# An output product as seven half-size float32 products in place of eight, in a fused mLSTM and SwiGLU kernel

## The chip, the cores and the metric

The kernel runs on one core of a Trainium2 chip. The metric is the device time of one execution in microseconds (us), the median over several runs; lower is better. All arithmetic of the block that is changed is float32.

## The reference

The first half is an mLSTM cell with 4 batches, 8 heads, 768 steps and head size 40; its result is laid out as 3072 tokens of 320 features. The second half, which the change touches, is a SwiGLU block over these tokens:

```python
# x: (3072, 320)   w_gate, w_val: (320, 1536)   w_out: (1536, 320)
g = x @ w_gate
silu = g * (1.0 / (1.0 + np.exp(-g)))
val = x @ w_val
return (silu * val @ w_out).astype(np.float32)
```

## The kernel before

The 768 steps are cut into six groups of 128 steps (`g` = 0 to 5). A group holds 128 steps of each of the 4 batches, so 512 tokens. For every group the kernel does three things on TensorE, in an order that is written out by hand (no scheduler moves instructions):

- **Hidden layer**, `hidden(g, m)` for m = 0 to 11: 128 of the 1536 inner features for all 512 tokens, gate and value side by side in two PSUM banks (line 651). ScalarE takes the silu into a tile `sg` (line 656, two buffers), VectorE multiplies by the value and writes `h_sb` (line 657). `h_sb` holds 13 blocks of 128 features by 512 tokens, and `hid` walks round these 13, so that a group writes other blocks than the last one.
- **mLSTM work of the next group** (`n` = g + 1), put between the hidden blocks by the table `slots`: scores, state, output of the cell, and, in slots 8 and 10, `send_squares`: 32 small DMAs that move the cell's result to `x_sq`, from where VectorE turns it into the next group's `xT` (`turn_inputs`, line 426, four instructions).
- **Output product**, `project(g, u)` for the four batches u: twelve float32 multiplications in a chain over the twelve feature blocks, each with 128 tokens as the stationary operand and 320 outputs as the moving one (line 667). ScalarE copies the bank out (line 661), SyncE sends it (line 662).

A float32 multiplication is executed as two TensorE passes, so the profile counts 2 MATMUL and 2 LDWEIGHTS records for each. Group 0's output product (`project_all`, line 674) is arranged differently and the change leaves it alone; with "the five later groups" g = 1 to 5 is meant.

Between the four `project` calls stands other work that runs on other engines. For f = g + 2 below 6 (g = 1 to 3) the decay weights `w_sb` are made ready: they are loaded by SyncE (line 447, slot 9), VectorE subtracts (`weights_sub`, line 451, two instructions), GpSimd masks (line 456, four), ScalarE takes exponents (line 460), GpSimd weighs the values (line 341). The four `turn_inputs` stand there too, for g = 1 to 4:

```python
        for u in range(B):
            if f < NG and u < 2:
                weights_sub(f, u)
                weights_mask(u)
...
            if n < NG and u >= 2:
                turn_inputs(n, 2 * u - 4)
                turn_inputs(n, 2 * u - 3)
            project(g, u)
```

Every engine works through its own instructions in the order in which the program issues them, and SyncE's DMA queue does so too. PSUM has four banks for the hidden layer and the output product (tag `gen`) and four for the cell.

Of the kernel before, what the change touches and what calls it, by code (L numbers as in the profile page):

```python
# [9 lines left out]
F32 = mybir.dt.float32  # L10
# [4 lines left out]
ALU = mybir.AluOpType  # L15
# [3 lines left out]
L = 128  # L19
# [5 lines left out]
def kernel(  # L25
# [18 lines left out]
    nc = tc.nc  # L44
    B, H, S, D = q.shape
    BH = B * H
    NG = S // L
# [5 lines left out]
    DM, DF = moe_w_gate.shape  # L53
    NFC = DF // 128
    TW = B * L
# [4 lines left out]
    NH = NFC + 1  # L60
# [6 lines left out]
    work = ctx.enter_context(tc.tile_pool(name="work", bufs=2))  # L67
# [8 lines left out]
    def bank(name, tag="cell"):  # L76
        return psum.tile([128, 512], F32, name=name, tag=tag)

    def half(i):
        return slice(i * SUB, (i + 1) * SUB)  # L80
# [5 lines left out]
    def heads(P):  # L86
        return slice(P * UH, (P + 1) * UH)
# [13 lines left out]
    wo_sb = const.tile([128, NFC, DM], F32)  # L101
    h_sb = const.tile([128, NH, TW], F32)
# [237 lines left out]
    def weigh_values(eng, P):  # L340
        eng.tensor_tensor(vw_sb[:, heads(P)], v_sb[:, heads(P)], w_sb[:, heads(P), last].to_broadcast([128, UH, D1]),  # L341
                          op=ALU.mult)
# [82 lines left out]
    def turn_inputs(n, u):  # L425
        nc.vector.transpose(out=xT(n)[:, :, ts(u, L)], in_=x_sq[:, u * NKC:(u + 1) * NKC].rearrange("p w t d -> p w (t d)"))  # L426

    def xT(n):
        return xTs[max(n - 1, 0) % 2]
# [19 lines left out]
    def weights_sub(n, P):  # L449
        gb = g_T[:, n, heads(P)].unsqueeze(2).to_broadcast([128, UH, SUB])  # L450
        nc.vector.tensor_tensor(w_sb[:, heads(P)], gb, w_sb[:, heads(P)], op=ALU.subtract)  # L451

    def weights_mask(P):
        for i in range(2):
            w = w_sb[half(i), heads(P)]
            nc.gpsimd.affine_select(w, w, compare_op=ALU.is_ge, fill=NEG, base=0, pattern=[[0, UH], [1, SUB]],  # L456
                                    channel_multiplier=-1)

    def weights_exp(P):
        nc.scalar.activation(w_sb[:, heads(P)], w_sb[:, heads(P)], AF.Exp)  # L460

    def sig(P):
        nc.scalar.activation(o_sb[:, heads(P)], o_sb[:, heads(P)], AF.Sigmoid)
# [10 lines left out]
    A, V, G = nc.scalar, nc.vector, nc.gpsimd  # L474
# [166 lines left out]


    def hid(g, m):
        return h_sb[:, (g * NFC + m) % NH, :]

    def hidden(g, m, first=()):
        ps = [bank("gv_ps", "gen") for _ in range(2)]
        x = xT(g)
        for kc in range(NKC):
            for i in range(2):  # L650
                nc.tensor.matmul(ps[i], lhsT=wgv_sb[half(i), m, PAIRS[kc][i] if g < 2 else kc, :], rhs=x[half(i), kc, :],  # L651
                                 start=(kc == 0), stop=(kc == NKC - 1))
        for f in first:
            f()
        sg = work.tile([128, TW], F32, name="sg")
        nc.scalar.activation(sg, ps[0], AF.Silu)  # L656
        nc.vector.tensor_tensor(hid(g, m), sg, ps[1], op=ALU.mult)  # L657

    def result(g, u, p):
        z = work.tile([128, DM], F32, name="z_sb")  # L660
        nc.scalar.copy(z, p)  # L661
        nc.sync.dma_start(out=out[ds(u * S + g * L, L), :], in_=z)

    def project(g, u):
        p = bank("o_ps", "gen")[:, 0:DM]
        for m in range(NFC):
            nc.tensor.matmul(p, lhsT=hid(g, m)[:, ts(u, L)], rhs=wo_sb[:, m, :], start=(m == 0), stop=(m == NFC - 1))  # L667
        result(g, u, p)

    def project_all(g, after):  # L670
        ps = [bank("o_ps", "gen")[:, 0:DM] for _ in range(B)]
        for m in range(NFC):
            for u in range(B):
                nc.tensor.matmul(ps[u], lhsT=hid(g, m)[:, ts(u, L)], rhs=wo_sb[:, m, :], start=(m == 0),  # L674
                                 stop=(m == NFC - 1))
            for f in after.get(m, ()):
                f()
        for u in range(B):
            result(g, u, ps[u])

    live = {}

# [41 lines left out]
    run = lambda f, *a, **b: (lambda: f(*a, **b))  # L724
# [29 lines left out]
    def early_squares(part):  # L754
# [17 lines left out]
        11: [run(early_squares, 1)],  # L772
    }
    project_all(0, after)
    early_scope.close()
    late = ctx.enter_context(tc.tile_pool(name="late", bufs=1))
# [2 lines left out]
    k_sq = late.tile([128, PP, L // SQ, SQ], F32, name="k_sq")  # L779
    nc.gpsimd.memset(k_sq, 0.0)  # L780
    x_sq = late.tile([128, B * NKC, L // SQ, SQ], F32, name="x_sq")


    for g in range(1, NG):
        n, f = g + 1, g + 2
        slots = {m: [] for m in range(NFC)}
        if n < NG:
            if n > 2:
                slots[0] = [run(turn_squares, q_sq, qT)]
                slots[1] = [run(turn_squares, k_sq, kT)]  # L790
            slots[3] = [run(do_scores), run(do_weigh, 0)]
            slots[4] = [run(do_weigh, 1)]
            slots[4].append(run(do_decayed, 2 * n))
            slots[5] = [run(do_add, n), run(do_state, 2 * n)]
            slots[7] = [run(do_attend, n, 0), run(do_gather, n, 0)]
            slots[8] = [run(do_divide, n, 0), run(send_squares, 0)]
            slots[9] = [run(do_attend, n, 1), run(do_gather, n, 1)]
            slots[10] = [run(do_divide, n, 1), run(send_squares, 1)]
        if f < NG:
            slots[2] += [run(load_squares, q_sq, q, f), run(load_squares, k_sq, k, f)]  # L800
            slots[5].append(run(load_all, k_sb, k, f))
            slots[9] += [run(load_all, v_sb, v, f), run(weights_load, f)]
            slots[10].append(run(load_all, o_sb, o_gate, f))
        for m in range(NFC):
            hidden(g, m)
            for s in slots[m]:
                s()
        for u in range(B):
            if f < NG and u < 2:
                weights_sub(f, u)  # L810
                weights_mask(u)
            if f < NG and u == 2:
                weights_exp(0)
                weights_exp(1)
                sig(0)
                sig(1)
                weigh_values(nc.gpsimd, 0)
                weigh_values(nc.gpsimd, 1)
            if n < NG and u >= 2:
                turn_inputs(n, 2 * u - 4)  # L820
                turn_inputs(n, 2 * u - 3)
            project(g, u)


# [28 lines left out]
```

## Time and profile before

| | |
|---|---|
| median of 3 runs | 551.57 us (551.15 to 551.81) |
| span of the profiled execution | 550.0 us |
| TensorE matmul busy | 544.9 us, 99% of the span |
| VectorE, ScalarE, GpSimd busy | 236.1, 136.1 and 103.0 us |
| hidden layer, line 651 | 316.6 us busy, 1440 matmul records |
| output product of groups 1 to 5, line 667 | 130.5 us busy, 480 matmul records |
| output product of group 0, line 674 | 26.9 us busy, 96 matmul records |
| DMA | 45.69 MB, 83 GB/s mean |

No total time is recorded for the profiled execution itself; its span is 1.6 us (0.3%) under the median of the timed runs, which also hold what lies around the span.

A row of the costliest groups reads: line, engine, operation, written tile, read tiles, shapes (for TensorE rows of the array times columns of the array, then the moving operand), the number of records, then busy time and the mean duration of one record in ns, then the idle time ahead of them. PEld is TensorE's loading of the stationary operand. Records of neighbouring matmuls overlap, since the profile's duration of one covers its way through the array; so the pace is read from the distance between starts. A line of the timeline gives start and length in us of a run of like instructions, how many there are, and in brackets how long the engine sat idle before and for whom.

### The profile page before, as it was taken

How to read it: one execution, taken by the hardware profiler on the slowest of the kernel's cores; microseconds unless marked ns; L12 is line 12 of the kernel's file. 1: busy time of each engine (PE TensorE's matmuls, PEld its weight loads, DVE VectorE, ACT ScalarE, POOL GpSimd, SP SyncE). 2: the span in 40 equal slices, each digit the busy share in tenths (PEclk: the TensorE clock that was granted, in tenths of full speed). 3: DMA queues.
4: the chain of work that ended last, by engine and by line, in shares of the span. 5: the costliest groups of instructions: out<-in, count | busy, mean ns of one | idle time of the engine just before them, and what ended most of it. 6: DMA issues, size and time to landing. Idle time of an engine off the chain costs nothing.

```text
span 550.0 us, 11592 instructions
## 1 busy us (share of the span) xinstructions
PE 544.9 (99%) x4989; PEld 311.4 (57%) x4989; DVE 236.1 (43%) x397; ACT 136.1 (25%) x203; POOL 103.0 (19%) x95
## 2 busy tenths in 40 slices
PE   8999999999999999999999999999999999999997
PEld 4964556774555575545575545576455567444475
DVE  5778668961346232455421545531436621111100
ACT  4376755352110133011024101115110100111100
POOL 2304265673011060011133011124001100000000
PEclk9999999999999999999999999999999999999999
DMA  9999997878431762660564551395000131000000
GB/s 123 177 294 184 188 277 154 146 104 118 53 49 23 120 112 64 74 74 11 87 117 104 63 72 14 59 146 113 1 1 2 32 63 40 12 1 0 2 24 24
DMA packets 223994, 45.69 MB, mean 83 GB/s; under 512 B 214504, under 2 KB 219112, under 8 KB 223944
## 3 DMA queue, kind: packets, MB, share of 16 engines
q1 hardware_dynamic: 222036, 42.11, 46.7%
q10 hardware_dynamic: 1908, 2.85, 1.9%
q8 instruction: 39, 0.64, 0.5%
q14 instruction: 11, 0.09, 0.1%
HBM read 35.68 MB, written 4.01 MB: 72 GB/s over the span
## 4 chain that ended last, share of the span: by engine, by line
PE 98%; DVE 1%; ACT 0%; issue 0%; ACTq 0%; DVEq 0%
PE gv_ps L651 57%; PE o_ps L667 24%; PE o_ps L674 5%; PE inter L377 2%; PE sp L331 2%; PE intra L382 2%; PE add L353 1%; PE first_y L530 1%; PE burn L469 1%; PE tp_kq L509 1%; PE sp L519 1%; PE wps L480 0%; PE tp_kq L296 0%; PE wps L484 0%; PE wps L489 0%; PE tp_x L439 0%
## 5 line engine op out<-in xcount | busy, mean ns | idle before, releaser
L651 PE MATMUL gv_ps<-xT,wgv_sb 64*128 64x512 f32 x1440 | 316.6, 593 | 0.3 <-DVE wgv_sb L207 0.3
L651 PEld LDWEIGHTS gv_ps<-xT,wgv_sb 64*128 64x128 f32 x1440 | 138.1, 187 | 159.1 <-issue 156.4
L657 DVE TENSOR_TENSOR h_sb<-sg,gv_ps 128x512 f32<-128x512 f32 x72 | 49.5, 688 | 212.3 <-ACT sg L656 212.3
L667 PE MATMUL o_ps<-wo_sb,h_sb 128*128 128x320 f32 x480 | 130.5, 433 | 0.0
L667 PEld LDWEIGHTS o_ps<-wo_sb,h_sb 128*128 128x128 f32 x480 | 90.8, 190 | 41.0 <-issue 3.8
L656 ACT ACTIVATE sg<-gv_ps 128x512 f32<-128x512 f32 x72 | 43.0, 597 | 263.7 <-PE gv_ps L651 263.7
L456 POOL TENSOR_SCALAR_AFFINE_SELECT w_sb<-w_sb 64x1024 f32<-64x1024 f32 x20 | 28.5, 1423 | 63.9 <-DVE w_sb L451 62.9
L362 POOL TENSOR_TENSOR C<-C,dec 128x328 f32<-128x328 f32 x20 | 14.5, 738 | 134.8 <-DVE C L369 134.8
L661 ACT COPY z_sb<-o_ps 128x320 f32<-128x320 f32 x24 | 10.0, 423 | 93.2 <-PE o_ps L667 89.4
L403 POOL TENSOR_TENSOR o_sb<-o_sb,y_sb 128x640 f32<-128x640 f32 x10 | 14.2, 1431 | 78.9 <-DVE y_sb L394 78.9
L674 PE MATMUL o_ps<-wo_sb,h_sb 128*128 128x320 f32 x96 | 26.9, 437 | 0.0
L451 DVE TENSOR_TENSOR w_sb<-g_T,w_sb 128x1024 f32<-128x1024 f32 x10 | 13.1, 1354 | 28.6 <-DMA w_sb<-M_dram 28.6
L426 DVE STREAM_TRANSPOSE xT<-x_sq 128x640 f32<-128x640 f32 x16 | 12.5, 822 | 22.9 <-DMA x_sq<-x_sb 22.9
L674 PEld LDWEIGHTS o_ps<-wo_sb,h_sb 128*128 128x128 f32 x96 | 17.9, 190 | 7.2
L394 DVE TENSOR_TENSOR y_sb<-y_sb,intra 64x328 f32<-64x328 f32 x40 | 19.7, 492 | 0.7
L369 DVE TENSOR_TENSOR C<-C,add 40x328 f32<-40x328 f32 (+1 forms) x36 | 17.7, 493 | 1.2 <-POOL C L362 0.6
L377 PEld LDWEIGHTS inter<-C,qT 64*64 64x64 f32 x640 | 10.2, 134 | 7.3 <-issue 6.1
L460 ACT ACTIVATE w_sb<-w_sb 128x1024 f32<-128x1024 f32 x10 | 10.6, 1058 | 12.7 <-POOL w_sb L456 12.7
L207 POOL TENSOR_TENSOR wgv_sb<-wgv_sb,low 128x640 int32<-128x640 int32 x6 | 9.3, 1546 | 23.5 <-DVE wgv_sb L200 23.5
L341 POOL TENSOR_TENSOR vw_sb<-v_sb,w_sb 128x656 f32<-128x656 f32 x10 | 12.8, 1306 | 0.4
L338 DVE TENSOR_TENSOR w_sb<-sp,w_sb 128x512 f32<-128x512 f32 x20 | 12.7, 682 | 0.0
L397 DVE TENSOR_SCALAR den<-den 128x16 f32<-128x16 f32 x10 | 12.2, 1215 | 0.3
(132 smaller groups left out, 344.5 us busy)
## 6 DMA issues: line engine op xcount, KB each, us to landing
w_sb<-M_dram SPq DMA_DIRECT2D x10, 512.0 KB, 7.3
x_sq<-x_sb SPq DMA_DIRECT2D x128, 40.0 KB, 2.0
k_sb<-in_k_dram SPq DMA_DIRECT2D x12, 320.0 KB, 6.0
v_sb<-in_v_dram SPq DMA_DIRECT2D x12, 320.0 KB, 5.6
o_sb<-in_o_gate_dram SPq DMA_DIRECT2D x12, 320.0 KB, 5.5
raw<-in_moe_w_out_dram SPq DMA_DIRECT2D x3, 1280.0 KB, 7.5
out_dram<-z_sb SPq DMA_DIRECT2D x24, 160.0 KB, 1.8
q_sb<-in_q_dram SPq DMA_DIRECT2D x32, 64.0 KB, 2.3
```

What stands on the lines that cost most here:

```text
L362: nc.gpsimd.tensor_tensor(state(s + 1)[:, a], state(s)[:, a], dec[:, s - 2, a].unsqueeze(2).to_broadcast([128, UA, D1]), op=ALU.mult)
L369: nc.vector.tensor_tensor(c, c, ps[r], op=ALU.add)
L377: nc.tensor.matmul(inter[two][half(i), a, :], lhsT=qT[half(two), P * UA + a, half(i)], rhs=state(2 * n + i)[half(two), P * UA + a, :], sta ...
L394: nc.vector.tensor_tensor(t, t, intra[i][half(c)], op=ALU.add)
L403: eng.tensor_tensor(o, o, y[:, :, 0:D], op=ALU.mult)
L451: nc.vector.tensor_tensor(w_sb[:, heads(P)], gb, w_sb[:, heads(P)], op=ALU.subtract)
L456: nc.gpsimd.affine_select(w, w, compare_op=ALU.is_ge, fill=NEG, base=0, pattern=[[0, UH], [1, SUB]], channel_multiplier=-1)
L651: nc.tensor.matmul(ps[i], lhsT=wgv_sb[half(i), m, PAIRS[kc][i] if g < 2 else kc, :], rhs=x[half(i), kc, :], start=(kc == 0), stop=(kc == N ...
L656: nc.scalar.activation(sg, ps[0], AF.Silu)
L657: nc.vector.tensor_tensor(hid(g, m), sg, ps[1], op=ALU.mult)
L667: nc.tensor.matmul(p, lhsT=hid(g, m)[:, ts(u, L)], rhs=wo_sb[:, m, :], start=(m == 0), stop=(m == NFC - 1))
L674: nc.tensor.matmul(ps[u], lhsT=hid(g, m)[:, ts(u, L)], rhs=wo_sb[:, m, :], start=(m == 0), stop=(m == NFC - 1))
```

## The change

In groups 1 to 5 the output product is no longer four chains of twelve multiplications with 320 output columns. Tokens (batches 0 and 1 against 2 and 3), inner features (blocks 0 to 5 against 6 to 11) and outputs (columns 0 to 159 against 160 to 319) are each halved. The plain way then has eight half-size products; the new function `project_seven` computes seven products of sums of halves and adds the results up (a form of Strassen's and Winograd's scheme). Each product is 6 feature blocks times 2 batches, so 12 multiplications with a 128 by 128 stationary operand and 160 moving columns.

What is added for it:

- `out_weights`, once on GpSimd after group 0: three tiles of weight sums `wT`, and a difference in place in `wo_sb`.
- `out_sums(k)`, six times in each group on GpSimd, after hidden blocks 6 to 11: a sum into `S_lo` (or the thirteenth block of `h_sb`) and a difference in place of the second token half of block k.
- `out_second` and `out_fourth`, in each group three VectorE instructions each, which change the sums in place between the products that use them. The fifth product in the order of issue (`"b"`) reads what `out_second` writes, the seventh (`"d"`, second time) what `out_fourth` writes.
- Four VectorE additions, one on GpSimd and three ScalarE copies that put the results together, in place of four ScalarE copies; eight half-size output DMAs in place of four. Two `sg` buffers hold the partial results `u2` and `v`.

`hid` now gives block m in every group. The weights' and inputs' preparation is put between the seven products by `before`.

```diff
     def hid(g, m):
-        return h_sb[:, (g * NFC + m) % NH, :]
+        return h_sb[:, m, :]
-    def project(g, u):
-        p = bank("o_ps", "gen")[:, 0:DM]
-        for m in range(NFC):
-            nc.tensor.matmul(p, lhsT=hid(g, m)[:, ts(u, L)], rhs=wo_sb[:, m, :], start=(m == 0), stop=(m == NFC - 1))
-        result(g, u, p)
+    def out_weights(eng):
+        lo, hi = wo_sb[:, 0:KH], wo_sb[:, KH:]
+        n1, n2 = slice(0, NW), slice(NW, DM)
+        eng.tensor_tensor(wT[:, 0], lo[:, :, n2], lo[:, :, n1], op=ALU.subtract)
+        eng.tensor_tensor(wT[:, 1], hi[:, :, n2], wT[:, 0], op=ALU.subtract)
+        eng.tensor_tensor(wT[:, 2], hi[:, :, n1], wT[:, 1], op=ALU.subtract)
+        eng.tensor_tensor(lo[:, :, n2], hi[:, :, n2], lo[:, :, n2], op=ALU.subtract)
+    def out_sums(k, eng):
+        eng.tensor_tensor(s_sum(k), h_sb[:, k, second_half], h_sb[:, KH + k, second_half], op=ALU.add)
+        eng.tensor_tensor(h_sb[:, k, second_half], h_sb[:, k, first_half], h_sb[:, k, second_half], op=ALU.subtract)
+    def out_second(eng):
+        for j in range(KH // 2):
+            eng.tensor_tensor(s_pair(j), s_pair(j), h_sb[:, 2 * j:2 * j + 2, first_half], op=ALU.subtract)
+    def out_fourth(eng):
+        for j in range(KH // 2):
+            eng.tensor_tensor(s_pair(j), h_sb[:, KH + 2 * j:KH + 2 * j + 2, first_half], s_pair(j), op=ALU.subtract)
+    def project_seven(g, before):
...
+        def product(x, lhs, rhs, start, stop):
+            for k in range(KH):
+                for i in range(2):
+                    nc.tensor.matmul(node[x][:, i], lhsT=lhs(k)[:, ts(i, L)], rhs=rhs(k), start=start and k == 0 and i == 0,
+                                     stop=stop and k == KH - 1, skip_group_check=True)
...
+        step(0)
+        product("a", a11, lambda k: wo_sb[:, k, n1], True, False)
+        nc.scalar.copy(u2, node["a"])
+        step(1)
+        product("c", a21, lambda k: wo_sb[:, k, n2], True, False)
+        nc.scalar.copy(v, node["c"])
+        step(2)
+        product("d", s_sum, lambda k: wT[:, 0, k], True, False)
+        nc.vector.tensor_tensor(v, v, node["d"], op=ALU.add)
+        out_second(nc.vector)
+        step(3)
+        product("a", a12, lambda k: wo_sb[:, KH + k, n1], False, True)
+        z = fresh()
+        nc.scalar.copy(z, node["a"])
+        send(z, 0, n1)
+        step(4)
+        product("b", s_sum, lambda k: wT[:, 1, k], True, True)
+        nc.vector.tensor_tensor(u2, u2, node["b"], op=ALU.add)
+        out_fourth(nc.vector)
+        nc.gpsimd.tensor_tensor(v, v, u2, op=ALU.add)
+        send(v, 2, n2)
+        step(5)
+        product("c", a22, lambda k: wT[:, 2, k], False, True)
+        z = fresh()
+        nc.vector.tensor_tensor(z, u2, node["c"], op=ALU.add)
+        send(z, 2, n1)
+        step(6)
+        product("d", s_sum, lambda k: wo_sb[:, KH + k, n2], False, True)
+        nc.vector.tensor_tensor(u2, u2, node["d"], op=ALU.add)
+        send(u2, 0, n2)
...
+    out_weights(nc.gpsimd)
...
         for m in range(NFC):
             hidden(g, m)
+            if m >= KH:
+                out_sums(m - KH, nc.gpsimd)
...
+        before = {i: [] for i in range(7)}
+        if f < NG:
+            before[0] += [run(weights_sub, f, 0), run(weights_mask, 0)]
+            before[2] += [run(weights_sub, f, 1), run(weights_mask, 1)]
+            before[4] += [run(weights_exp, 0), run(weights_exp, 1), run(sig, 0), run(sig, 1),
+                          run(weigh_values, G, 0), run(weigh_values, G, 1)]
+        if n < NG:
+            before[4] += [run(turn_inputs, n, 0), run(turn_inputs, n, 1)]
+            before[6] += [run(turn_inputs, n, 2), run(turn_inputs, n, 3)]
+        project_seven(g, before)
```

More of the change, by code (lines that the diff above doesn't have):

```diff
@@ L679, in project_all, with s_sum, s_pair @@
             result(g, u, ps[u])
+    KH = NFC // 2
+    NW = DM // 2
+    TH = TW // 2
+    first_half, second_half = slice(0, TH), slice(TH, TW)
+    def s_sum(k):
+        return S_lo[:, k] if k < 4 else h_sb[:, NFC].rearrange("p (k t) -> p k t", t=TH)[:, k - 4]
+    def s_pair(j):
+        return S_lo[:, 2 * j:2 * j + 2] if j < 2 else h_sb[:, NFC].rearrange("p (k t) -> p k t", t=TH)
+    def out_weights(eng):
[5 more added lines that the diff above has]
+        eng.tensor_tensor(lo[:, :, n2], hi[:, :, n2], lo[:, :, n2], op=ALU.subtract)
@@ new lines, in project_seven, with send, fresh, step @@
+    def project_seven(g, before):
+        n1, n2 = slice(0, NW), slice(NW, DM)
+        a11 = lambda k: h_sb[:, k, first_half]
+        a12 = lambda k: h_sb[:, KH + k, first_half]
+        a21 = lambda k: h_sb[:, k, second_half]
+        a22 = lambda k: h_sb[:, KH + k, second_half]
+        node = {x: bank("o_ps", "gen")[:, 0:DM].rearrange("p (u d) -> p u d", d=NW) for x in "acdb"}
+        kept = {x: work.tile([128, TW], F32, name="sg")[:, 0:DM].rearrange("p (u d) -> p u d", d=NW) for x in "uv"}
+        def send(z, u, n):
+            for i in range(2):
+                nc.sync.dma_start(out=out[ds((u + i) * S + g * L, L), n], in_=z[:, i])
+        def fresh():
+            return work.tile([128, DM], F32, name="z_sb").rearrange("p (u d) -> p u d", d=NW)
+        def product(x, lhs, rhs, start, stop):
+            for k in range(KH):
+                for i in range(2):
+                    nc.tensor.matmul(node[x][:, i], lhsT=lhs(k)[:, ts(i, L)], rhs=rhs(k), start=start and k == 0 and i == 0,
+                                     stop=stop and k == KH - 1, skip_group_check=True)
+        def step(n):
+            for f in before.get(n, ()):
+                f()
+        u2, v = kept["u"], kept["v"]
+        step(0)
[28 more added lines that the diff above has]
+        send(u2, 0, n2)
@@ L781 @@
     x_sq = late.tile([128, B * NKC, L // SQ, SQ], F32, name="x_sq")
+    wT = late.tile([128, 3, KH, NW], F32, name="wT")
+    S_lo = late.tile([128, 4, TH], F32, name="S_lo")
+    out_weights(nc.gpsimd)
     for g in range(1, NG):
@@ L805 @@
             hidden(g, m)
+            if m >= KH:
+                out_sums(m - KH, nc.gpsimd)
             for s in slots[m]:
                 s()
[L808 to L822, printed above, removed]
+        before = {i: [] for i in range(7)}
[8 more added lines that the diff above has]
+        project_seven(g, before)
 _INS = ['q', 'k', 'v', 'i_gate', 'f_gate', 'o_gate', 'moe_w_gate', 'moe_w_val', 'moe_w_out']
```

## The prediction

> **What bounds the kernel now.** I read the page first: busy shares, the clock by slices, and the chain of work that ended last.
>
> ```profile
> PE 544.9 (99%) x4989; PEld 311.4 (57%) x4989; DVE 236.1 (43%) x397; ACT 136.1 (25%) x203; POOL 103.0 (19%) x95
> PEclk9999999999999999999999999999999999999999
> PE 98%; DVE 1%; ACT 0%; issue 0%; ACTq 0%; DVEq 0%
> ```
>
> TensorE is the bound, without gaps and at full clock, so TensorE time taken away counts in full unless TensorE then has to wait. The groups by cost give the row that changes and its weight loads:
>
> ```profile
> L667 PE MATMUL o_ps<-wo_sb,h_sb 128*128 128x320 f32 x480 | 130.5, 433 | 0.0
> L667 PEld LDWEIGHTS o_ps<-wo_sb,h_sb 128*128 128x128 f32 x480 | 90.8, 190 | 41.0 <-issue 3.8
> ```
>
> A weight load's record is 190 ns long. What happens to it when a pass lasts only half as long is the first question. Records overlap, so I read paces from starts, in the timeline of short windows:
>
> ```profile
> 189.59 5.82 PE L667 MATMUL o_ps<-wo_sb,h_sb 128*128 128x320 f32 x21
> 211.64 4.89 PE L651 MATMUL gv_ps<-xT,wgv_sb 64*128 64x512 f32 x22
> 25.23 1.76 PE L530 MATMUL first_y<-v_sb,h_sb 128*128 128x41 f32 x15
> 26.93 1.29 PE L564 MATMUL tp_x<-ident,x_sb 128*128 128x128 f32 x10
> 54.71 0.53 PE L638 MATMUL dec_ps<-dec_r,halves 32*128 32x160 f32 x2
> ```
>
> The second question is what stands on the other engines during the output product. This is the timeline of group 1's, and VectorE's same wait in groups 2 and 3:
>
> ```profile
> 184.64 26.11 PE L667 MATMUL o_ps<-wo_sb,h_sb 128*128 128x320 f32 x96
> 185.37 0.69 DVE L657 TENSOR_TENSOR h_sb<-sg,gv_ps 128x512 f32<-128x512 f32 x1 [2.80 <-ACT sg L656]
> 186.66 3.58 SPq L447 DMA_DIRECT2D w_sb<-M_dram  x2
> 195.84 2.36 DVE L451 TENSOR_TENSOR w_sb<-g_T,w_sb 128x1024 f32<-128x1024 f32 x2 [9.78 <-DMA w_sb<-M_dram]
> 197.18 5.64 POOL L456 TENSOR_SCALAR_AFFINE_SELECT w_sb<-w_sb 64x1024 f32<-64x1024 f32 x4 [17.67 <-DVE w_sb L451]
> 198.11 1.56 DVE L426 STREAM_TRANSPOSE xT<-x_sq 128x640 f32<-128x640 f32 x2
> 202.91 2.57 POOL L341 TENSOR_TENSOR vw_sb<-v_sb,w_sb 128x656 f32<-128x656 f32 x2
> 204.10 1.57 DVE L426 STREAM_TRANSPOSE xT<-x_sq 128x640 f32<-128x640 f32 x2 [4.42 <-DMA x_sq<-x_sb]
> 282.31 2.36 DVE L451 TENSOR_TENSOR w_sb<-g_T,w_sb 128x1024 f32<-128x1024 f32 x2 [10.13 <-DMA w_sb<-M_dram]
> 367.00 2.36 DVE L451 TENSOR_TENSOR w_sb<-g_T,w_sb 128x1024 f32<-128x1024 f32 x2 [8.71 <-DMA w_sb<-M_dram]
> ```
>
> VectorE sits idle about 10 us until the weights `w_sb` land, because SyncE's queue still pushes out the x_sq transfers. Today nobody needs VectorE in that time.
>
> **TensorE, removed and added.** Removed in each group: 48 multiplications, 96 passes. Their pace is (5.82 − 0.433) / 20 = 0.2694 us, so 25.86 us; from 184.64 to the next hidden block at 210.68 it is 26.04 us, so 0.18 us go into the two changes of shape. Added: 84 multiplications, 168 passes of 160 columns. The pace of 512 columns (pairs in two row halves) is (4.89 − 0.593) / 10 = 0.429 us; with 0.2694 for 320 that is 0.83 ns a column, and 160 columns get 0.2694 − 160 × 0.00083 = 0.136 us, if the load stays hidden. Is it? L530 loads 128x128 float32 for each pass and moves only 41 columns: its pace, (1.76 − 0.283) / 14 = 0.106 us, is the most that such a load can need when nothing hides it. L564, with 128 moving columns and a full load each, goes at (1.29 − 0.273) / 9 = 0.113 us. Both are under 0.136, and the 320-column row shows no load on top of its movement. So the 190 ns are mostly latency and I take 0.136. Bounds: 0.1347 (half of 0.2694) below; above, the single pair L638, which has 160 columns and whose second pass starts 0.53 − 0.294 = 0.24 us after the first, load unhidden (320-column chains pay that only in their first step, in the 0.18). New stage: 168 × 0.136 + 0.18 = 23.05 us. Gain 2.99 us a group, 14.9 us in five.
>
> [...]
>
> **VectorE, a new wait.** In the new order the two `weights_sub` stand ahead of `v += d` and of `out_second`, and the fifth product cannot start before the first of `out_second`'s three instructions is done. Times from the start of the stage: the products take 168 / 7 × 0.136 = 3.27 us each, so the fifth could start at 0.1 + 4 × 3.27 = 13.2. The first `weights_sub` starts at 195.84 − 184.64 = 11.20 in group 1, 282.31 − 270.76 = 11.55 in group 2 and 367.00 − 356.87 = 10.13 in group 3 (270.76 and 356.87 are where those stages start). The next instruction follows 2.27 later (198.11), so `v += d` starts at 13.47; it delays the next by 0.41 (two 320-column additions, L409, take 0.89 in all, 0.49 for one); `out_second`'s first takes 0.69, as L657, and ends at 14.57. With 0.1 us for the load that now lies open, TensorE restarts at 14.7: 1.5 us lost, by the same steps 1.85 in group 2 and 0.45 in group 3, 3.8 in sum. The other two pairs, 0.6 us apart, stay ahead of a product that takes 1.09 us for a pair. Queued behind the waiting VectorE are two `turn_inputs` (1.56) and `u2 += b`: the turns fit into the fifth product. Groups 4 and 5 have no `weights_sub` and no wait. Bounds: 0, if the weights land 2 us sooner; twice, if these instructions go slower beside GpSimd's masks. Against the latter: the second L451 and L426 run beside the masks at their usual pace.
>
> **The end.** Now the last copy (0.43) and one DMA follow the last pass. Then: an addition of 0.49, and two DMAs, of which the second is issued 0.38 us later (0.33 to issue and the semaphore); a 160-column pass leaves the array 0.13 us sooner. Together +0.3 us.
>
> **What I cost at nothing, and its cover.** `out_sums`: L362 takes 738 ns for 328 columns and L403 1431 for 640, so 0.58 for 256; twelve make 6.9 us of GpSimd in 50 us of hidden layer. The last pair ends about 2.7 us into the stage; its reader, the end of the second product, comes at 6.1. Without that cover it is 3.4 us later per group. `out_weights`: four instructions of 960 columns, 8.6 us on GpSimd from 126.8; first used at 188. L362, queued behind it, moves from 126.8 to 135.5; L369 adds to its result after 152. `out_fourth`: 0.41 + 0.69 after the fifth product, under the sixth (3.27). The last two turns: x_sq lands 19.5, 20.2 and 18.8 us into the stage, they run behind `z = u2 + c` at 21.5 and end at 23.5, and the hidden layer wants them at 24.6; 1 us of slack, and each further us is paid. `v += u2` on GpSimd stands behind masks and L341 and ends near 21.5, before `u2 += d` at 24.6. Four more DMA issues cost SyncE 4 × 0.38 = 1.5 us; behind them stand the next group's loads, which wait for VectorE's turns (L321) anyway. The last send frees the `sg` buffer some 3 us into the next hidden block, whose silu comes at 4.4.
>
> **The sum.** −14.9 + 3.8 + 0.3 = −10.8 us. The profiled span of 550.0 becomes 539.2; the median stands 1.6 above the span (551.57), so 540.8, say 541.0 us.
>
> **Rivals.**
> - *Weight loads come to the surface (slower).* Place: the gap between passes. It decides from (26.04 − 0.18) / 168 = 0.154 us a pass. At the 0.190 of the load's record the stage takes 168 × 0.190 + 0.18 = 32.1 us, +6.1 a group; the wait on VectorE vanishes, since the fifth product then comes at 18: 551.6 + 30.3 + 0.3 = 582 us. At L638's 0.24 it would be 624. For it: the 190 ns and L638. Against: L530 and L564.
> - *VectorE held up by GpSimd.* L397, a 16-column instruction, takes 1.2 us beside L403 on GpSimd. If `v += d` and `out_second` each had to wait for one mask (1.42), the last pair would be ready at 13.5 + 4 × 1.42 = 19.2, the product end near 20.3 instead of 18.0, 2.3 us in three groups: 548 us.
> - *No wait at all*, weights landing earlier: 551.6 − 14.9 + 0.3 = 537 us.
>
> **How the numbers follow.** Main case, 538 to 545: 0.77. No wait: 0.08. Held up: 0.06. Loads at the surface: 0.07, mostly slower; it gives "within 0.2%" (about what a measurement of this kernel can tell from no change) 0.02. The range runs from 536.5, below the no-wait case, to 549: the held-up case, or passes of 0.142 (+5 us) with twice the wait.
>
> **What would show it.** In the profile after: L725 with 840 records at a pace of 136 ns; stages of about 24.6, 24.9, 23.5, 23.1 and 23 us; a wait of TensorE for VectorE's `S_lo` from L700, once in groups 1 to 3, none in 4. A pace above 154 ns, a wait ahead of the seventh product or of the next hidden block would prove me wrong.

## The result and the profile after

The changed kernel takes 545.96 us (median of 4, 545.21 to 546.26) against 551.69 us on the same chip; the ratio is 0.9887, with a 95% interval of 0.9873 to 0.9901. The profiled execution took 546.09 us with a span of 544.3 us, 5.7 us less than the span before.

On the page, the busy shares, the clock by slices and the chain that ended last:

```profile
PE 533.7 (98%) x5349; PEld 339.0 (62%) x5349; DVE 281.9 (52%) x447; ACT 134.2 (25%) x198; POOL 169.6 (31%) x164
PEclk9999999999999989999999999999999999999999
PE 86%; SPq 7%; DVE 4%; DMA 1%; issue 1%; ACT 0%; DVEq 0%
```

TensorE is busy for 11 us less, but it no longer makes up the chain alone: some 12% of it now runs over SyncE's queue, VectorE and DMAs. The clock line has an 8 a little after a third of the span. The five output stages (start:end, length, busy times, granted clock after the POOL column) show where:

```profile
core 0: us, PE busy (x) PEld busy (x) DVE busy (x) ACT busy (x) POOL busy (x), PEclk, DMA share, GB/s
184.20:211.26 27.06, 25.04 (x171) 24.43 (x169) 15.35 (x16) 8.03 (x10) 14.02 (x11) 0.94 0.81 133
271.48:296.67 25.19, 23.89 (x170) 22.95 (x169) 15.47 (x16) 8.03 (x10) 14.02 (x11) 1.00 0.85 140
356.96:382.43 25.47, 23.89 (x171) 22.95 (x169) 15.47 (x16) 8.03 (x10) 14.03 (x11) 1.00 0.83 138
442.71:465.73 23.02, 23.02 (x171) 22.85 (x169) 9.39 (x14) 1.87 (x4) 2.64 (x3) 1.00 0.25 51
517.43:540.36 22.93, 22.93 (x170) 22.85 (x168) 6.43 (x10) 1.87 (x4) 2.64 (x3) 1.00 0.08 22
```

Groups 4 and 5 lost 3 us each, as the multiplications say. Groups 1 to 3 kept little of it: group 1's stage is 1 us longer than before. TensorE's timeline in groups 1 and 2, from the end of the fourth product:

```profile
194.08 3.42 PE L725 MATMUL o_ps<-wo_sb,h_sb 128*128 128x160 f32 x24
199.52 4.04 PE L725 MATMUL o_ps<-wT,S_lo 128*128 128x160 f32 x16 [2.02 <-DVE S_lo L700]
203.36 4.71 PE L725 MATMUL o_ps<-wT,h_sb 128*128 128x160 f32 x32
...
281.37 3.42 PE L725 MATMUL o_ps<-wo_sb,h_sb 128*128 128x160 f32 x24
285.70 1.35 PE L725 MATMUL o_ps<-wT,S_lo 128*128 128x160 f32 x8 [0.91 <-DVE S_lo L700]
287.24 1.35 PE L725 MATMUL o_ps<-wT,S_lo 128*128 128x160 f32 x8 [0.19 <-DVE S_lo L700]
288.78 4.61 PE L725 MATMUL o_ps<-wT,h_sb 128*128 128x160 f32 x32 [0.18 <-DVE h_sb L700]
```

The bracket names the releaser: L700, `out_second`. In group 2 TensorE waits three times, once for each pair of sums. In group 1 it waits 2.0 us once, and then 16 passes last 4.04 us where 16 passes otherwise last 2.34: from 200.34 on the records stand 0.267 us apart, half the pace. The same columns as above, for the 3.41 us before that moment and the 3.41 us after it:

```profile
196.93:200.34 3.41, 1.39 (x11) 1.15 (x10) 3.41 (x4) 1.71 (x2) 3.35 (x2) 1.00 0.37 60
200.34:203.75 3.41, 3.41 (x14) 3.21 (x14) 3.41 (x4) 1.22 (x2) 3.20 (x4) 0.50 0.36 59
```

The granted clock is 0.50 in the second. This is VectorE's timeline in that time, group 1:

```profile
195.57 2.36 DVE L451 TENSOR_TENSOR w_sb<-g_T,w_sb 128x1024 f32<-128x1024 f32 x2 [9.95 <-DMA w_sb<-M_dram]
197.85 0.48 DVE L741 TENSOR_TENSOR sg<-sg,o_ps 128x320 f32<-128x320 f32 x1
198.24 1.22 DVE L700 TENSOR_TENSOR S_lo<-S_lo,h_sb 128x512 f32<-128x512 f32 x1
199.39 1.62 DVE L700 TENSOR_TENSOR S_lo<-S_lo,h_sb 128x512 f32<-128x512 f32 x1
200.93 1.62 DVE L700 TENSOR_TENSOR h_sb<-h_sb 128x512 f32<-128x512 f32 x1
```

GpSimd's timeline in the same time:

```profile
196.92 2.01 POOL L456 TENSOR_SCALAR_AFFINE_SELECT w_sb<-w_sb 64x1024 f32<-64x1024 f32 x1 [9.69 <-DVE w_sb L451]
199.00 1.48 POOL L456 TENSOR_SCALAR_AFFINE_SELECT w_sb<-w_sb 64x1024 f32<-64x1024 f32 x1
200.54 1.47 POOL L456 TENSOR_SCALAR_AFFINE_SELECT w_sb<-w_sb 64x1024 f32<-64x1024 f32 x1
```

The two engines take turns. The first mask ends at 198.93, the first L700 at 199.46, 0.53 later; the second mask ends at 200.48, the second L700 at 201.01, again 0.53 later; the third mask ends at 202.01, the third L700 at 202.55, 0.54 later. The other way round the second mask ends 1.02 us after the first L700 and the third 1.00 after the second, where the shortest mask of this profile takes 1.14 in all. So in these rows each waits for the other's whole instruction. In groups 4 and 5, without masks, the same L700 takes 0.69 us. Not all VectorE instructions take part: L741, which reads one operand from PSUM, is 0.48 us long in the middle of the first mask.

### The profile page after: what moved, and what is told of

The parts are those of the page before. It is cut to its first block, busy times and chain, and to the rows that moved or that the text cites. A ratio compares the mean times of both kernels' runs of the same rounds, so it can differ in the third digit from the quotient of the medians.

```text
span 544.3 us, 12484 instructions
## 1 busy us (share of the span) xinstructions
PE 533.7 (98%) x5349; PEld 339.0 (62%) x5349; DVE 281.9 (52%) x447; ACT 134.2 (25%) x198; POOL 169.6 (31%) x164
## 4 chain that ended last, share of the span: by engine, by line
PE 86%; SPq 7%; DVE 4%; DMA 1%; issue 1%; ACT 0%; DVEq 0%
PE gv_ps L651 55%; PE o_ps L725 14%; PE o_ps L668 5%; SPq L422 4%; SPq L447 2%; PE sp L331 2%; PE inter L377 2%; PE add L353 2%; PE intra L382 2%; DMA x_sq<-x_sb 1%; PE first_y L530 1%; DVE S_lo L700 1%; PE burn L469 1%; DVE w_sb L451 1%; SPq L117 1%
## 5 line engine op out<-in xcount | busy, mean ns | idle before, releaser
L725 PEld LDWEIGHTS o_ps<-wo_sb,h_sb 128*128 128x128 f32 x400 | 55.0, 190 | 3.8 <-issue 3.8
L725 PE MATMUL o_ps<-wo_sb,h_sb 128*128 128x160 f32 x400 | 57.3, 300 | 0.0
L456 POOL TENSOR_SCALAR_AFFINE_SELECT w_sb<-w_sb 64x1024 f32<-64x1024 f32 x20 | 31.4, 1572 | 38.8 <-DVE w_sb L451 37.9
L695 POOL TENSOR_TENSOR S_lo<-h_sb 128x256 f32<-128x256 f32 x20 | 15.2, 761 | 88.1 <-DVE h_sb L657 88.1
L725 PE MATMUL o_ps<-wT,S_lo 128*128 128x160 f32 x160 | 25.8, 315 | 4.5 <-DVE S_lo L700 4.5
L725 PE MATMUL o_ps<-wT,h_sb 128*128 128x160 f32 x200 | 29.2, 301 | 0.4 <-DVE h_sb L700 0.4
L725 PEld LDWEIGHTS o_ps<-wT,h_sb 128*128 128x128 f32 x200 | 28.0, 192 | 0.9 <-DVE h_sb L700 0.9
L451 DVE TENSOR_TENSOR w_sb<-g_T,w_sb 128x1024 f32<-128x1024 f32 x10 | 13.1, 1354 | 27.9 <-DMA w_sb<-M_dram 27.9
L725 PEld LDWEIGHTS o_ps<-wT,S_lo 128*128 128x128 f32 x160 | 23.5, 198 | 5.9 <-DVE S_lo L700 5.9
L668 PE MATMUL o_ps<-wo_sb,h_sb 128*128 128x320 f32 x96 | 26.9, 437 | 0.0
L696 POOL TENSOR_TENSOR h_sb<-h_sb 128x256 f32<-128x256 f32 x30 | 22.8, 759 | 2.3
L668 PEld LDWEIGHTS o_ps<-wo_sb,h_sb 128*128 128x128 f32 x96 | 17.9, 190 | 7.2
L207 POOL TENSOR_TENSOR wgv_sb<-wgv_sb,low 128x640 int32<-128x640 int32 x6 | 9.3, 1543 | 23.5 <-DVE wgv_sb L200 23.5
L695 POOL TENSOR_TENSOR h_sb<-h_sb 128x256 f32<-128x256 f32 x10 | 8.0, 797 | 24.5 <-DVE h_sb L657 24.5
```

The costliest lines, as they stand in the source:

```text
L695: eng.tensor_tensor(s_sum(k), h_sb[:, k, second_half], h_sb[:, KH + k, second_half], op=ALU.add)
L696: eng.tensor_tensor(h_sb[:, k, second_half], h_sb[:, k, first_half], h_sb[:, k, second_half], op=ALU.subtract)
L725: nc.tensor.matmul(node[x][:, i], lhsT=lhs(k)[:, ts(i, L)], rhs=rhs(k), start=start and k == 0 and i == 0, stop=stop and k == KH - 1, skip ...
```

## The experiments

**Theory.** The missing 5 us are VectorE's: `out_second` stands in its queue behind `weights_sub`, which waits for `w_sb`, and then takes turns with the masks; in group 1 the 2.02 us of idle time also halved TensorE's clock, for 3.41 us. **Rivals:** the half-size passes are dear by themselves; the wait would only move if the order were changed; the half clock has another cause.

**The half-size shape alone.** The kernel before, with its output product cut into eight half-size products and no sums:

```diff
+    def project_half(g, j):
+        t, n = 2 * (j // 2), slice((j % 2) * DM // 2, (j % 2 + 1) * DM // 2)
+        p = bank("o_ps", "gen")[:, 0:DM].rearrange("p (u d) -> p u d", d=DM // 2)
+        for m in range(NFC):
+            for i in range(2):
+                nc.tensor.matmul(p[:, i], lhsT=hid(g, m)[:, ts(t + i, L)], rhs=wo_sb[:, m, n], ...)
...
-            project(g, u)
+            project_half(g, u)
```

> The kernel before with its output product of groups 1 to 5 cut into eight half-size products (96 multiplications of 160 columns in place of 48 of 320), without any sums: the shape of the change without its saving. Theory (a pass of 160 columns costs 0.136 us, the weight load stays hidden, the whole gain is 168 passes in place of 192): a stage takes 192 x 0.136 + 0.18 = 26.3 us against 26.04, and two DMAs at the end cost 0.4 us: 551.7 + 1.3 + 0.4 = 553.4 us. Rival (the half-size shape itself gains or loses, for instance by earlier release of banks or by open weight loads at the bank changes): under 551 or over 555 us.

It took 554.17 us, ratio 1.0035 (1.0021 to 1.0048). TensorE's timeline of group 1's stage, which starts and ends with a hidden block:

```profile
184.67 26.35 PE L675 MATMUL o_ps<-wo_sb,h_sb 128*128 128x160 f32 x192
210.94 1.56 PE L651 MATMUL gv_ps<-xT,wgv_sb 64*128 64x512 f32 x6
```

The stage is 26.27 us, as reckoned from 0.136 us a pass; the median is 0.8 us above the expectation. The shape alone brings nothing (a stage is 0.23 us longer than before); the saving is 168 passes in place of 192.

**The order on VectorE.** Both `weights_sub` and the masks go behind `out_second`:

```diff
-            before[0] += [run(weights_sub, f, 0), run(weights_mask, 0)]
-            before[2] += [run(weights_sub, f, 1), run(weights_mask, 1)]
+            before[3] += [run(weights_sub, f, 0), run(weights_mask, 0), run(weights_sub, f, 1), run(weights_mask, 1)]
```

> The two weights_sub on VectorE and the four masks on GpSimd are issued after out_second (step 3) instead of before it (steps 0 and 2); nothing else changes. [...] Rival A (the wait only moves: out_fourth now runs beside the masks and holds the seventh product): 1 to 1.5 us of wait there in groups 1 to 3, about 542 us. Rival B (the loss has nothing to do with the order on VectorE): no change, 546 us.

By the theory, as put on record before the run, `out_second` would run at 0.69 us each right after the third product, TensorE would not wait ahead of the fifth, the stages of groups 1 to 3 would take 23.1 to 23.5 us at a clock of 1.000, and the median would be about 538 us (537.5 to 539).

540.94 us, ratio 0.9794 (0.9778 to 0.9811): 5 us better than the changed kernel, 3 us short of the theory's number. TensorE's timeline of this kernel, from group 2's stage:

```profile
282.19 2.34 PE L725 MATMUL o_ps<-wT,S_lo 128*128 128x160 f32 x16
...
292.98 2.42 PE L651 MATMUL gv_ps<-xT,wgv_sb 64*128 64x512 f32 x10 [0.62 <-DVE xT L426]
```

And VectorE's timeline of the same kernel, from group 3's stage:

```profile
370.34 3.19 DVE L704 TENSOR_TENSOR S_lo<-h_sb,S_lo 128x512 f32<-128x512 f32 x2
373.45 1.79 DVE L704 TENSOR_TENSOR h_sb<-h_sb 128x512 f32<-128x512 f32 x1
375.16 0.47 DVE L757 TENSOR_TENSOR z_sb<-sg,o_ps 128x320 f32<-128x320 f32 x1
375.56 1.56 DVE L426 STREAM_TRANSPOSE xT<-x_sq 128x640 f32<-128x640 f32 x2
```

The wait ahead of the fifth product is gone (its 16 passes follow with no bracket) and the clock is 1.00 in all stages. Now `out_fourth` runs beside the masks and GpSimd's weighing, at 1.6 to 1.8 us each, and the last `turn_inputs` behind it come late: TensorE waits 0.6 us for `xT`, in all three groups; these stages are 23.9 us long. So Rival A was right that a part moves, but the seventh product lost only 0.24 us, and the hidden layer behind it the rest.

**No masks.** The order of the changed kernel, the masks of these stages left out, with what follows for the decay weights as the expectation says:

```diff
-            before[0] += [run(weights_sub, f, 0), run(weights_mask, 0)]
-            before[2] += [run(weights_sub, f, 1), run(weights_mask, 1)]
+            before[0] += [run(weights_sub, f, 0)]
+            before[2] += [run(weights_sub, f, 1)]
```

> The GpSimd masks of the output stages (groups 1 to 3) are left out, so the decay weights keep entries that should be zero; the order on VectorE stays as in the changed kernel. Theory (out_second is slow because it takes turns with the masks): out_second runs at 0.69 us instead of 1.2 to 1.6; TensorE's wait ahead of the fifth product shrinks to what the late w_sb alone makes of it, about 1.4, 0.4 and 0.6 us in groups 1 to 3, with no waits between its pairs; no half clock; about 541 to 542 us. Rival (VectorE's in-place instructions are slow for another reason, the order alone makes the wait): out_second stays at 1.2 to 1.6 us, 546 us.

540.87 us, ratio 0.9802 (0.9780 to 0.9824). VectorE's timeline of this kernel in group 2:

```profile
279.12 2.36 DVE L451 TENSOR_TENSOR w_sb<-g_T,w_sb 128x1024 f32<-128x1024 f32 x2 [8.93 <-DMA w_sb<-M_dram]
281.40 0.48 DVE L741 TENSOR_TENSOR sg<-sg,o_ps 128x320 f32<-128x320 f32 x1
281.80 1.29 DVE L700 TENSOR_TENSOR S_lo<-S_lo,h_sb 128x512 f32<-128x512 f32 x2
283.00 0.69 DVE L700 TENSOR_TENSOR h_sb<-h_sb 128x512 f32<-128x512 f32 x1
```

And TensorE's timeline of the same kernel:

```profile
282.54 2.44 PE L725 MATMUL o_ps<-wT,S_lo 128*128 128x160 f32 x16 [0.46 <-DVE S_lo L700]
```

Without the masks every L700 is 0.69 us again, and the two waits between the pairs are gone. What is left is the wait for the late `w_sb`: by the spacing of passes 1.2, 0.6 and 1.0 us. The theory holds, and the two halves of the loss (order, taking turns) are told apart: these three stages are 24.31, 23.77 and 24.09 us long, together 3.1 us above the 23.02 of group 4, where those of the changed kernel stood 8.7 above it. The order alone cost 3.1; the turns, with the half clock behind them, cost the rest.

**Both at once, and the best version.** One `weights_sub` with its masks behind `out_second`, the other behind `out_fourth`, so that masks run beside neither:

```diff
-            before[0] += [run(weights_sub, f, 0), run(weights_mask, 0)]
-            before[2] += [run(weights_sub, f, 1), run(weights_mask, 1)]
-            before[4] += [run(weights_exp, 0), run(weights_exp, 1), run(sig, 0), run(sig, 1),
-                          run(weigh_values, G, 0), run(weigh_values, G, 1)]
+            before[3] += [run(weights_sub, f, 0), run(weights_mask, 0)]
+            before[4] += [run(weights_exp, 0)]
+            before[5] += [run(weights_sub, f, 1), run(weights_mask, 1)]
+            before[6] += [run(weights_exp, 1), run(sig, 0), run(sig, 1),
+                          run(weigh_values, G, 0), run(weigh_values, G, 1)]
```

> The first weights_sub with its two masks is issued after out_second (step 3), the second with its two after out_fourth (step 5), so that no mask runs beside either set of VectorE instructions; the exponents and weighed values follow (exponent 0 in step 4, the rest in step 6). Theory (two full SBUF inputs on VectorE take turns with GpSimd): out_second at 0.69 us each, out_fourth at 0.69 but for one turn with the addition on GpSimd (0.7 us more), the last two turn_inputs end before the seventh product, no TensorE wait of over 0.1 us in any stage: stages of 23.0 to 23.2 us, about 538.3 us. Rival (the order after out_second is enough, what is left in the first reordering is the late x_sq): TensorE still waits for xT by 0.6 us in groups 1 to 3, about 540.5 us.

537.13 us (536.73 to 537.47), ratio 0.9728 (0.9712 to 0.9745), 1.2 us better than expected and the fastest of all. Its stages:

```profile
184.71:207.73 23.02, 23.02 (x171) 22.85 (x169) 11.58 (x16) 4.21 (x6) 7.00 (x7) 1.00 0.85 132
267.81:290.82 23.01, 23.01 (x170) 22.84 (x168) 11.58 (x16) 4.21 (x6) 6.94 (x7) 1.00 0.88 136
350.91:373.93 23.02, 23.02 (x171) 22.85 (x169) 11.57 (x16) 4.21 (x6) 6.95 (x7) 1.00 0.87 136
```

Groups 1 to 3 now equal group 4, so no wait for `xT` is left either, and the rival of the late `x_sq` falls. VectorE's busy time in a stage is 11.6 us instead of 15.4: nearly 4 us of it had been waiting for GpSimd.

**The half clock.** First a filler: four spare multiplications ahead of the fifth product, to shorten the idle time.

```diff
         step(4)
+        if g < 4:
+            spare = bank("burn")
+            for _ in range(4):
+                nc.tensor.matmul(spare[:, 0:NW], lhsT=ident, rhs=wT[:, 0, 0], start=True, stop=True)
         product("b", s_sum, lambda k: wT[:, 1, k], True, True)
```

> The changed kernel with four spare multiplications of 160 columns (8 passes, 1.09 us, result unused) put on TensorE ahead of the fifth product in groups 1 to 3, where TensorE waits. Theory (the half clock of 3.4 us in group 1 comes from TensorE's 2.0 us of idle time): idle time is 0.9 us at most, no pass at 0.267 us, the granted clock is 1.000 in every run, the stage of group 1 falls from 27.1 to 25.2 us and groups 2 and 3 stay within 0.3 us: about 544.3 us. Rival (the half clock has another cause, such as load or a moment in time): passes at 0.267 us remain in group 1 and the median stays near 546 us.

545.23 us, ratio 0.9879 (0.9865 to 0.9894), 0.9 us above the expectation; clocks 0.999 to 1.000 in four executions, no slow passes in the one profiled. That agrees with the theory but does not settle it, since the changed kernel does not show the half clock every time either, and because `w_sb` landed 1.3 us later here in group 3, with 1.4 us of idle time left behind the filler (more than the 0.9 expected). So the kernel as it is was run again:

> The changed kernel as it is, once more, for the clock of more executions. Theory (idle time halves the clock, by chance of when it falls): 0.997 in some executions and 1.000 in others, those with 0.997 longer by about 1 us; median 546 us. Rival (a state of that chip or moment): all at 1.000, near 545.2 us.

545.21 us, ratio 0.9880 (0.9866 to 0.9895). Clocks 0.999, 0.996, 0.999 and 1.000; with the first four that is three executions of eight at 0.996 or 0.997, at 546.1 to 546.3 us, and five at 0.999 or 1.000, at 544.8 to 545.8. In the one profiled here TensorE was idle for 1.3 us in group 1, and the clock stayed up:

```profile
199.23 1.35 PE L725 MATMUL o_ps<-wT,S_lo 128*128 128x160 f32 x8 [1.33 <-DVE S_lo L700]
```

`weights_sub` started 0.7 us sooner there than in the execution with 2.0 us of idle time. So this profile shows a shorter wait that kept the clock, and not a wait of 2.0 us that did; whether the other executions that kept it had shorter waits, or longer ones at a better moment, stays open. Next the idle time made longer, by one VectorE transpose ahead of `out_second`:

```diff
         nc.vector.tensor_tensor(v, v, node["d"], op=ALU.add)
+        if g < 4:
+            x = xT(g).rearrange("p c t -> p (c t)")
+            nc.vector.transpose(out=x[:, 0:2 * TW], in_=x[:, 2 * TW:4 * TW])
         out_second(nc.vector)
```

> The changed kernel with one more VectorE instruction ahead of out_second in groups 1 to 3, a transpose of 1024 columns between dead parts of the old xT (1.2 us, single input, its result is not used): the wait of TensorE ahead of the fifth product grows to about 3.1, 2.0 and 2.4 us. Theory (an idle time of about 2 us can halve the clock): passes at 0.267 us, for 3.4 us, after the wait in one to three of these stages, granted clock 0.991 to 0.997, and 546.0 + 3 x 1.0 + 1 to 3 times 1.8 less what the slower products hide: 549 to 552 us. [...]

550.85 us (549.2 to 551.91, ten executions), ratio 0.9974 (0.9962 to 0.9987). The clock was below 0.998 in all ten: 0.994 in eight, 0.997 and 0.989 in one each. Had idle time nothing to do with it, a clock of 0.999 to 1.000 and 548.5 to 549.5 us were expected. The stages of the profiled one, that with 0.989:

```profile
184.16:212.17 28.01, 24.82 (x170) 24.40 (x169) 15.75 (x17) 8.03 (x10) 13.98 (x11) 0.94 0.79 129
272.39:299.94 27.55, 25.14 (x170) 24.33 (x168) 15.74 (x17) 8.03 (x10) 13.97 (x11) 0.94 0.79 129
360.22:388.27 28.05, 25.22 (x171) 24.57 (x169) 15.74 (x17) 8.03 (x10) 13.96 (x11) 0.94 0.74 126
```

And TensorE's timeline behind the three waits:

```profile
200.66 3.97 PE L725 MATMUL o_ps<-wT,S_lo 128*128 128x160 f32 x16 [3.19 <-DVE S_lo L700]
288.10 4.04 PE L725 MATMUL o_ps<-wT,S_lo 128*128 128x160 f32 x16 [2.40 <-DVE S_lo L700]
376.17 1.35 PE L725 MATMUL o_ps<-wT,S_lo 128*128 128x160 f32 x8 [2.64 <-DVE S_lo L700]
```

All three stages lost clock after 2.4 to 3.2 us of idle time. One instruction of 1.2 us, three times, cost 5 us. The theory holds: idle time of TensorE is the cause. But by an estimate not every such wait cost clock: 3.41 us at half clock take 0.3% off the mean, so a mean of 0.994 stands for two such stretches, and 0.997 for one.

The clock records in the trace of the changed kernel show one thing more: 194.560 us at full clock, 3.413 at half, 341.333 at full, which is 57 times, once and 100 times 3.413 us. In the kernel before, the one stretch at full clock lasts 546.132 us, 160 times as much. The half clock began 0.8 us after TensorE was back at work. So it may matter where on this grid a wait falls; no run here was made to test that.

## Why the prediction was right, and where it was wrong

The sign and the range held; the gain was 5.7 us where 10.8 were forecast. 545.96 us lies above the 538 to 545 that were given 0.77, and so above the main case even with twice the wait. It is within the range because the range reached up to the held-up case, and because the half clock, which no case held, cost only some 1.8 us: in part that is luck. (The other case that was named for the top, passes of 0.142 us with twice the wait, adds up to 549.8, not to 549.) By the steps:

- **The multiplications: right.** The pace is 0.136 us a pass, and the stage without waits 23.02 us (23.05 forecast; 168 × 0.136 + 0.18 is 23.03). From 26.04 that is 3.0 us a group, 15 in five. The weight loads stayed hidden: their records are 190 to 198 ns long on the mean, with a full load for each pass and a pass every 0.136 us. The 582 or 624 us of the rival that brought them to the surface were not seen.
- **The wait on VectorE: right in place and cause, mis-sized.** It was put at 3.8 us; the three stages stand 4.04 + 2.17 + 2.45 = 8.7 us above 23.02. By the spacing of passes: 2.2, 1.1 and 1.35 us ahead of the fifth product, 1.4 us between its pairs, about 0.7 us for loads that lay open after each wait (8 passes behind a wait last 1.35 us, others 1.25), and some 1.8 us of half clock in group 1. The first `weights_sub` started 11.37, 10.26 and 10.53 us into the stages, where 11.20, 11.55 and 10.13 were forecast; that alone makes 0.7 us less wait. The step that failed is the duration of `out_second`. Its three instructions took 1.22, 1.6 and 1.6 us: the first made the wait ahead of the fifth product 0.5 us longer in each group, the other two put a wait ahead of the second and the third pair in groups 2 and 3, where one wait was forecast and three came. I took 0.69 us each and set the taking of turns aside because "the second L451 and L426 run beside the masks at their usual pace". L426 reads one input and took 1.56 us for two beside the masks as elsewhere. L451 held its pace (2.36 us for two), but the mask beside it did not: in the kernel before, the first mask, which started while the second L451 was running, was 2.01 us long and the second 1.14, so one of the two engines had waited. I had read the four masks as one merged line. The rival "held up by GpSimd" had the mechanism and was given 0.06; it had `v += d` wait too, which did not happen (L741, 0.48 us). The first two masks of group 1 in the kernel before:

```profile
197.18 2.01 POOL L456 TENSOR_SCALAR_AFFINE_SELECT w_sb<-w_sb 64x1024 f32<-64x1024 f32 x1 [17.67 <-DVE w_sb L451]
199.26 1.14 POOL L456 TENSOR_SCALAR_AFFINE_SELECT w_sb<-w_sb 64x1024 f32<-64x1024 f32 x1
```

- **The half clock: not foreseen.** I asked what a wait costs, not what comes after it.
- **The end: +0.5 us, forecast +0.3.** From the start of the last pass to the end of the span it is 4.08 us instead of 3.58. Three of the four hidden stages between the output stages grew by 0.14 to 0.21 us, 0.55 in sum, which I had at nothing. All of it lies in the multiplications of line 353 (the state), which last 1.74 to 1.81 us there instead of 1.60; I did not find out what they wait for. The first of the five stages began 0.4 us sooner (184.20 against 184.64; 184.16 to 184.91 in the other runs), which I take for scatter. In sum 15.0 − 8.7 − 0.5 − 0.55 + 0.4 gives the 5.7 us of the spans.
- **What was costed at nothing** held otherwise, though `out_sums` took 0.73 us each instead of 0.58 and each instruction of `out_fourth` 1.1 to 1.8 in groups 1 to 3 instead of 0.69: no wait ahead of the second or the seventh product, none of over 0.1 us ahead of the next hidden block.

L700, which reads both of its operands from SBUF, took 0.69 us without and 1.2 to 1.6 us with the masks. That the two engines take turns is measured; what they take turns for, no run shows.

## What to carry to other kernels

When sums are put on VectorE to save multiplications, look at what stands ahead of them in its queue and at what GpSimd does at that moment (one sum took 0.69 us alone and up to 1.6 us beside the masks); the same seven products gave 5.7 or 14.9 us, by where two VectorE instructions stand with the GpSimd and ScalarE work that follows them. Before a duration is taken from a row, look whether its neighbours on the other engine were stretched, one instruction at a time. A wait on the bounding engine is to be priced with the clock that may be lost behind it, here 3.41 us at half clock after 2.02 us of idle time.

## What was new of the hardware

TensorE's granted clock fell to 0.50 for 3.41 us after 2.02 us of idle time in one profiled execution, and not after 0.91 and 1.19 us in the same one, 1.33 us when the kernel was run again, and 1.37 us with the filler; with 2.4 to 3.2 us it fell in all three stages of the profiled run, to a mean of 0.94 in each. So 2.02 us were enough in the one profile that has such a wait.
